# Dummy products in planned idle time, port locks for table steps, and new seeds in an attention and expert-layer kernel

## The chip, the cores and the metric

The kernel runs on one core of a Trainium2 chip. The metric is the device time of one execution in microseconds (us). Three runs of the kernel before took 742.20, 740.81 and 737.13 us: the median is 740.81. The core has TensorE (PE, matrix products into the eight PSUM banks), VectorE (DVE), ScalarE (ACT), GpSimd (POOL) and SyncE (SP, which here issues most DMAs).

## The reference

Four batches of 576 tokens go through windowed attention (8 heads of 64, each token sees itself and the 63 before it), then through a layer of eight experts of which each token takes one, then through a dense layer with a tanh form:

```python
scores = scale * np.matmul(q, k.transpose(0, 1, 3, 2))       # q, k, v: (4, 8, 576, 64)
mask = (rel >= 0) & (rel < 64)
attn = softmax(np.where(mask, scores, -1e9)); x = np.matmul(attn, v)   # -> (2304, 512)
logits = x @ w_gate + modality_bias[modality_id]             # 8 experts
e_idx = np.argmax(logits, axis=1); gate_w = softmax(logits)[e_idx]
for e in range(8):                                           # tokens of expert e
    out[mask] = gate_w[mask, None] * (np.maximum(x[mask] @ w1[e], 0.0) @ w2[e])
h = out @ w_in                                               # (512, 2048)
y = (h - np.tanh(h)) @ w_out
```

## The kernel before

**Attention.** The 32 heads are handled as 16 pairs, four of each batch, and a tail per batch for the last 64 tokens. For each pair PE transposes keys and queries (L618), writes the mask and the scores into two banks (L731, L744), DVE takes row maxima (`nm`, L811), ACT the exponentials (`P`, L818), PE transposes them (L769) and multiplies with the values (L783). ACT or DVE copy each step's result out of PSUM.

**Routing.** After a batch's attention `route` computes the gate logits (L940), their maximum and its index, ranks of the tokens within their expert (L996 to L1000), and scales the token rows (`xr`, L921 and L923), which SP writes to memory (`xs`, L907). One-hot matrices `ob` and `rhs` are multiplied (L1068), and DVE adds the product to the table `T` of token numbers (L1076). `early_table` (after batches 0 and 2) and `unit_table` (after batch 3) turn counts into lists of work units by some dozens of DVE steps on one partition (L1118 to L1252).

**Expert stream.** Five units of up to 504 tokens follow. Units 0 and 1 are two lists of the expert that is the largest in batch 0, and start before attention has ended. For each, POOL gathers the rows (`xg`, L1349), PE transposes them (L618 with `xg`), ACT and DVE split them into two parts `xh` and `xl`; SP loads the weights (`raw`, L1415 and L1421), which are split into `wh` (ACT, POOL or DVE) and `wl` (DVE, at times POOL, L1440). The first products are L1465, the second L1485: 96 of each, all on PE.

**Dense layer.** From 326 us on, PE works at the dense layer (L1872 and L1920); its order is fixed by hand and the change does not touch it.

**What sets the order.** Each engine executes its instructions in one fixed order. Up to the end of the expert stream this order comes from a planner, `Flow`, that runs when the kernel is built: each step is an `Op` with an engine, a duration that the planner assumes, the steps that it waits for, the PSUM banks that it may take and a priority. The planner takes step after step, each at the earliest planned time, and the instructions are written out in this order. Where several steps could go, the lowest priority value goes first, plus a pseudo-random `nudge` whose seed is taken from `SEEDS`: one per batch for the priorities 0 to 20, the last for the rest. The time that the plan holds for a step has no effect on the chip: there only the order on each engine and the waits for data, buffers and banks remain.

`Flow.held` keeps a planned DVE step with `lock=True` from overlapping a planned POOL step, and the other way round. Steps without the lock are planned as if DVE and POOL never met:

```python
o = dict(DVE="POOL", POOL="DVE").get(e)
if o is None or (e == "DVE" and not op.lock):
    return t
a, b = self.hold[o]
return b if a < t + op.eng[e] and t < b else t
```

At the kernel's start `warm` puts nine products of the identity `idB` (128x128 with 128x512, L563) on PE while the first loads are under way.

Of the kernel before, what the change touches and what calls it, by code (L numbers as in the profile page):

```python
# [8 lines left out]
F32 = mybir.dt.float32  # L9
# [9 lines left out]
B, H, S, D = 4, 8, 576, 64  # L19
# [21 lines left out]
EB = (0, 2)  # L41
# [13 lines left out]
PACK = {("k", pi) for pi in range(1, LEND - 1)}  # L55
DQ = 0.62
SPACE = 2.0
NUDGE, SEEDS = 1.0, (17, 17, 88, 60, 17)
TURN, STICK = 0.095, 1.0
CONV0 = 14  # L60
CONVT, CONVP = 122.0, 5.1
SLACK = 8.0
# [94 lines left out]
class Flow:  # L157
# [6 lines left out]
    def __init__(self):  # L164
        self.free = dict(PE=5.8, DVE=5.0, ACT=5.0, POOL=8.0, SP=1.6)
        self.wire, self.th, self.n, self.floor = 0.0, [], 0, 0.0
        self.form = "full"
        self.hold = dict(DVE=(0.0, 0.0), POOL=(0.0, 0.0))
        self.bank = [Tok(0.0) for _ in range(8)]

# [46 lines left out]
    def pick(self):  # L217
# [22 lines left out]
        _, s, th = min((x for x in best[e] if x[0] <= lo), key=lambda x: prio(x[2]))  # L240
        return e, s + self.turn(e, th[3]), th

    def run(self):
        while self.th:
            e, s, th = self.pick()
            op, r = th[3], Done()
            r.e, r.s, r.rel = e, s, [g.take() for g in op.rings]
            r.t = s
            if e:
                end = s + op.eng[e]  # L250
                self.free[e] = end
                if e == "PE":
                    self.form = op.form
                if e == "POOL" or (e == "DVE" and op.lock):
                    self.hold[e] = s, end
                r.t = end + self.LAG[e]
                if op.wire:
                    self.wire = max(self.wire, end) + op.wire
                    r.t = self.wire + op.lag
                elif e == "POOL" and op.lag > 2:  # L260
                    r.t = end + op.lag
            else:
                th[4] = s
            if op.bank is not None:
                free = sorted((b for b in op.bank if self.bank[b].t is not None), key=lambda b: self.bank[b].t)
                r.bs = free[: op.nb]
                r.bts = [Tok() for _ in r.bs]
                r.bt = r.bts[0]
                for b, t in zip(r.bs, r.bts):
                    self.bank[b] = t  # L270
            r.tok = Tok(r.t)
            self.step(th, r)


class Kernel:
# [128 lines left out]
    def front(self):  # L404

        nc, f = self.nc, self.flow
# [52 lines left out]
            f.add(self.t_xsplit(i), -1)  # L459
        for n, t in enumerate(ORDER):  # L460
            f.add(self.t_conv(n, t), 1000 + n)
        f.run()
        self.psP_es.close()

# [92 lines left out]
    def behind(self, r):  # L557
        return r.s < self.gathered + 3.0

    def warm(self):  # L560
        ps = self.psP.tile([128, 512], F32, name="bank5").rearrange("p (a b) -> p a b", b=128)
        for i in range(9):
            self.nc.tensor.matmul(  # L563
                ps, self.idB, self.idB[:, None, :].to_broadcast([128, 4, 128]), start=True, stop=True
            )
# [366 lines left out]
    def route(self, b):  # L932
        nc, rt = self.nc, self.rt
        t0, t1, n = RT * b, RT * b + RT, RT
        o0 = (b % 2) * S
        for hf in range(2):
            r = yield Op(("PE", 0.49), self.tks("O", range(5 * b, 5 * b + 5)), bank=self.bankX, form="heads")
            ps = self.bt(r, 128, 288)
# [14 lines left out]
        r = yield Op(("DVE", 0.4), self.tks("P", [(5 * b + p, h) for p in range(4) for h in range(2)]), lock=True)  # L953
# [3 lines left out]
        r = yield Op(("PE", 0.075 * n), toks + [r.tok], bank=self.bankX, nb=2, form="rows")  # L957
        ps = [self.bt(r, 128, n, 64, i=k) for k in range(2)]
# [3 lines left out]
        r = yield Op(("DVE", 0.7), [r.tok], lock=True)  # L962
# [3 lines left out]
        for k in range(2):  # L966
# [4 lines left out]
                op=ALU.mult,  # L971
# [3 lines left out]
        r = yield Op(("DVE", 1.0), lock=True)  # L975
# [4 lines left out]
        r = yield Op(("ACT", 0.28), [r.tok])  # L980
# [3 lines left out]
        r = yield Op(("DVE", 0.95), lock=True)  # L984
# [9 lines left out]
        r = yield Op(("PE", 0.3), [to], bank=self.bankX)  # L994
# [14 lines left out]
        r = yield Op(("DVE", 0.5), [te], lock=True)  # L1009
# [7 lines left out]
        r = yield Op(("DVE", 0.35), [tp], lock=True)  # L1017
# [7 lines left out]
        r = yield Op(("DVE", 1.2), [tp], lock=True)  # L1025
# [5 lines left out]
        a = rt.tile([128, n], F32, name="ra")  # L1031
# [9 lines left out]
        tb = r.tok  # L1041
        ob = rt.tile([128, n, BR], BF16, name="ob")
        obp = rt.tile([128, n, BR], BF16, name="obp")
        sb = [128, n, BR]
        r = yield Op(("DVE", 0.72), [tb])
        nc.vector.tensor_tensor(
            ob, self.iobr[:, None, :].to_broadcast(sb), bm[:, :, None].to_broadcast(sb), op=ALU.is_equal
        )
        r = yield Op(("ACT", 0.72), [r.tok])
        nc.scalar.activation(obp, ob, AF.Copy, scale=self.pcol)  # L1050
        tobp = r.tok
        rhs = rt.tile([128, n, E, NSLOT], BF16, name="rhs")
        sr = [128, E, NSLOT]
        for i in range(n):
            r = yield Op(dict(DVE=0.3, POOL=0.45), bias=dict(DVE=0.6))
            self.eng(r).tensor_tensor(
                rhs[:, i],
                oh[:, i, :, None].to_broadcast(sr),
                eqa[:, i, None, :].to_broadcast(sr),
                op=ALU.mult,  # L1060
            )
        r = yield Op(dict(DVE=0.75, POOL=1.1), [tobp], bias=dict(DVE=0.8))
        self.eng(r).tensor_tensor(ob, ob, self.tbase[:, t0:t1, None].to_broadcast(sb), op=ALU.mult)
        r = yield Op(("PE", 0.14 * n), [r.tok], bank=self.bankX)
        pT, bk = self.bt(r, BR, E * NSLOT), r.bt
# [9 lines left out]
        r = yield Op(("DVE", 0.25), [r.tok])  # L1075
# [32 lines left out]
    def early_table(self, j, tc):  # L1108
# [2 lines left out]
        v = nc.vector  # L1111
        n = yield from self.counts("nA", tc)
        sh = [1, E]
        r = yield Op(("DVE", 1.6 if j == 0 else 0.6))
        t = rt.tile(sh, F32, name="et")
        mx = rt.tile([1, 1], F32, name="emx")
        if j == 0:
# [24 lines left out]
        if j == 0:  # L1142
# [2 lines left out]
                self.ei[0:1, 0:1], engines=[mybir.EngineType.SP], min_val=0, max_val=E - 1,  # L1145
                skip_runtime_bounds_check_because="an index of the eight experts by its making",
            )
        r = yield Op(("DVE", 0.7), [self.tk("TT", EB[j])])
        k = nc.values_load(
            self.ei[0:1, 1 + j : 2 + j], engines=[mybir.EngineType.DVE], min_val=0, max_val=E * NSLOT - CB,  # L1150
            skip_runtime_bounds_check_because="24 times an expert's index and 4 * j or less",
# [12 lines left out]
    def unit_table(self, tc):  # L1164
# [9 lines left out]
            v.tensor_reduce(c, a, op=ALU.add, axis=AX.X)  # L1174
            return c

        yield Op(("DVE", 1.1), prio=-1)
        s = cum(n, "cs0")
        st = rt.tile(sh, F32, name="st")
        v.tensor_tensor(st, s, n, op=ALU.subtract)  # L1180
# [2 lines left out]
        v.tensor_tensor(  # L1183
            g, n[:, :, None].to_broadcast(s3), self.jC[:, None, :].to_broadcast(s3), op=ALU.is_gt
        )
        yield Op(("DVE", 1.3), prio=-1)
        nu = rt.tile(sh, F32, name="nu")
        v.tensor_reduce(nu, g, op=ALU.add, axis=AX.X)
        j0 = rt.tile(sh, F32, name="j0")
# [2 lines left out]
        cu = cum(nu, "cs1")  # L1192
        cj = rt.tile(sh, F32, name="cj")
        v.tensor_tensor(cj, cu, nu, op=ALU.subtract)
        yield Op(("DVE", 1.0), prio=-1)
        v.tensor_tensor(cj, j0, cj, op=ALU.subtract)
        kb = rt.tile(sh, F32, name="kb")
        v.scalar_tensor_tensor(kb, cj, float(CB), self.e24, op0=ALU.mult, op1=ALU.add)
# [4 lines left out]
        v.tensor_tensor(  # L1203
            le, cu[:, None, :].to_broadcast(su), self.u1[:, :, None].to_broadcast(su), op=ALU.is_le
        )
        yield Op(("DVE", 1.2), prio=-1)
        eu = rt.tile([1, NLIST], F32, name="eu")
        v.tensor_reduce(eu, le, op=ALU.add, axis=AX.X)
        v.tensor_scalar(eu, eu, float(E - 1), None, op0=ALU.min)
# [7 lines left out]
        v.tensor_copy(tab[:, 0, :], eu)  # L1217
        for i, (base, step, cap) in enumerate(((kb, self.uB, E * NSLOT - CB), (cb, self.uC, NT))):
            w = le
            r3 = yield Op(("DVE", 1.3), prio=-1)  # L1220
            v.tensor_tensor(w, ou, base[:, None, :].to_broadcast(su), op=ALU.mult)
            r = rt.tile([1, NLIST], F32, name=f"tr{i}")
            v.tensor_reduce(r, w, op=ALU.add, axis=AX.X)
            v.tensor_tensor(r, r, step, op=ALU.add)
            v.tensor_scalar(tab[:, 1 + i, :], r, float(cap), 0.0, op0=ALU.min, op1=ALU.max)
            rs = r
        self.tab = tab
        for m in range(NSTAT):
            yield Op(("SP", 0.6), [r3.tok])
            u = Unit(None, CL if m == NSTAT - 1 else C)  # L1230
            u.e = self.list_reg(slice(m, m + 1), 0)
            x = yield Op(("DVE", 0.7), [self.tk("TT", B - 1)])
            self.unit(NEARLY + m, u, self.list_reg(slice(m, m + 1), 1), self.T, x.t, NRT)
        yield Op(("DVE", 1.8))
        fin = self.cp.tile([1, 2 + NEARLY], I32, name="fin")
        over = rt.tile([1, 1], F32, name="over")
        v.tensor_scalar(over, rs[:, NSTAT - 1 : NSTAT], float(NT - CL), None, op0=ALU.is_lt)
# [9 lines left out]
            v.tensor_scalar(d, r, float(C * j - NT), None, op0=ALU.add)  # L1247
            v.tensor_scalar(fin[:, 1 + j : 2 + j], d, self.evl[:, j : j + 1], float(NT), op0=ALU.mult, op1=ALU.add)
        self.fin = fin
        r = yield Op(("DVE", 0.2))  # L1250
        okB = self.cp.tile([1, 1], BF16, name="okB")
        v.tensor_scalar(okB, over, float(NSTAT), None, op0=ALU.is_le)  # L1252
        self.tk("table").t = r.t
# [823 lines left out]
```

## Time and profile before

| | |
|---|---|
| median of three runs | 740.81 us (737.13 to 742.20) |
| profiled execution | 739.21 us |
| its span, first to last instruction | 737.4 us |
| PE / DVE / ACT / POOL busy | 97% / 78% / 69% / 42% of the span |
| mean granted TensorE clock | 0.985 |
| expert stream's first product | 103.55 us |
| dense layer | from about 326 us to about 730 us |

A time on an engine's row is measured from the span's start. The granted clock is a share of 2.4 GHz: 1.00 is that level, 0.50 is 1.2 GHz, and a mean between them over a stretch says how much of it was spent at each. "Idle before" is time in which the engine had nothing to execute, with what ended it behind the arrow.

### The profile page before, as it was taken

To read this page: it belongs to the slowest core of one execution; us is meant where nothing else is said; L and a number is where in the kernel's file an instruction comes from. 1 tells how busy PE (TensorE), PEld (TensorE's weight loads), DVE (VectorE), ACT (ScalarE), POOL (GpSimd) and SP (SyncE) were. 2 spreads that over 40 slices of the span, in tenths; PEclk is the share of its full clock that TensorE was granted. 3 is DMA by queue.
4 is the path that set the end of the run, shared out by engine and by line. 5 is a ranking of instruction groups with operands and counts; after the bars stand their busy time and mean duration, and the time that the engine had idled before them with its cause. 6 is when DMAs were issued, how large, how long until landed. Compare 5 with 4: busy or idle time off the path is not lost.

```text
span 737.4 us, 15072 instructions
## 1 busy us (share of the span) xinstructions
PE 712.3 (97%) x5235; PEld 617.1 (84%) x5235; DVE 573.3 (78%) x1084; ACT 508.8 (69%) x1255; POOL 306.3 (42%) x359
## 2 busy tenths in 40 slices
PE   7889989899999999999999999999999999999995
PEld 4778777688888888999988899998989999899994
DVE  5887997979899887749999996767677676757663
ACT  5987884547666665748877776676767766767672
POOL 5455655653424322216774452434234333423222
PEclk9998999999999999999999999999999999999998
DMA  9987947687886966640010110101010000001001
GB/s 191 223 190 175 206 130 204 183 240 225 254 263 211 286 211 231 187 111 2 13 33 0 44 37 8 43 12 33 0 44 22 22 15 29 23 1 44 1 1 47
DMA packets 119251, 77.34 MB, mean 105 GB/s; under 512 B 54968, under 2 KB 112332, under 8 KB 119166
## 3 DMA queue, kind: packets, MB, share of 16 engines
q1 hardware_dynamic: 114822, 66.38, 32.6%
q0 software_dynamic: 3264, 9.63, 4.3%
q8 instruction: 43, 0.70, 0.4%
q10 hardware_dynamic: 1080, 0.28, 0.2%
q14 instruction: 42, 0.34, 0.2%
HBM read 62.10 MB, written 14.16 MB: 103 GB/s over the span
## 4 chain that ended last, share of the span: by engine, by line
PE 74%; DVE 12%; issue 4%; DMA 3%; ACT 2%; POOL 2%; SPq 2%; POOLq 0%; DVEq 0%; ACTq 0%
PE ps_q L1920 21%; PE ps_g L1872 21%; PE bank L1485 14%; PE bank L1465 12%; DVE gv L1893 2%; DVE gv L1892 2%; DMA va<-in_v 2%; PE bank L783 1%; PE bank L618 1%; DMA kr<-in_k 1%; DVE nm L811 1%; SPq L530 1%; PE bank L769 1%; DVE gv L1890 1%; ACT gs L1887 1%
## 5 line engine op out<-in xcount | busy, mean ns | idle before, releaser
L1903 POOL TENSOR_TENSOR gl<-gv,gh 128x384 fp32r<-128x384 f32 x95 | 102.4, 1078 | 167.0 <-ACT gh L1902 165.0
L1920 PE MATMUL ps_q<-H,gl 128*128 128x512 f32 x288 | 113.6, 394 | 0.7 <-POOL gl L1903 0.7
L1920 PE MATMUL ps_q<-H,gh 128*128 128x512 f32 x288 | 113.3, 393 | 0.0
L1890 DVE SCALAR_TENSOR_TENSOR gv<-gu,ps_g 128x384 f32<-128x384 f32 x94 | 51.7, 550 | 79.1 <-ACT gt L1885 78.7
L1902 ACT ACTIVATE gh<-gv 128x384 fp32r<-128x384 f32 x96 | 50.2, 523 | 89.1 <-issue 85.5
L1894 DVE COPY_PREDICATED gv<-gm,gt 128x384 f32<-128x384 int32 x96 | 77.7, 809 | 9.9
L1893 DVE SCALAR_TENSOR_TENSOR gv<-gs,gv 128x384 f32<-128x384 f32 x96 | 68.0, 708 | 10.0
L1440 DVE TENSOR_TENSOR wl<-raw,wh 128x512 fp32r<-128x512 f32 x77 | 59.8, 795 | 9.1 <-ACT wh L397 8.7
L1920 PEld LDWEIGHTS ps_q<-H,gl 128*128 128x128 f32 x288 | 54.0, 188 | 15.1 <-POOL gl L1903 2.6
L1886 ACT ACTIVATE gs<-gu,pa 128x384 f32<-128x384 f32 x96 | 59.2, 616 | 8.7 <-DVE gv L1892 8.7
L1887 ACT ACTIVATE gs<-gu,pa 128x384 f32<-128x384 f32 x96 | 58.9, 613 | 7.8 <-DVE gv L1893 7.7
L1892 DVE SCALAR_TENSOR_TENSOR gv<-gs,gv 128x384 f32<-128x384 f32 x96 | 64.0, 666 | 0.0
L1920 PEld LDWEIGHTS ps_q<-H,gh 128*128 128x128 f32 x288 | 54.0, 188 | 8.6 <-ACT gh L1902 0.3
L1889 ACT ACTIVATE gm<-gu,pth 128x384 f32<-128x384 f32 x96 | 58.4, 609 | 0.0
L1891 DVE TENSOR_TENSOR gt<-ps_g,gt 128x384 f32<-128x384 f32 x94 | 51.7, 550 | 0.0
L1884 ACT ACTIVATE gu<-ps_g 128x384 f32<-128x384 f32 x94 | 44.5, 473 | 1.6 <-PE ps_g L1872 1.6
L1885 ACT ACTIVATE gt<-ps_g 128x384 f32<-128x384 f32 x94 | 45.4, 483 | 0.0
L397 ACT ACTIVATE ys<-bank 128x504 f32<-128x504 f32 (+1 forms) x20 | 11.1, 557 | 46.1 <-PE bank L1485 30.3
L397 ACT ACTIVATE wh<-raw 128x512 fp32r<-128x512 f32 x69 | 41.7, 624 | 0.0
L1465 PE MATMUL bank<-xl,wh 128*128 128x504 f32 (+1 forms) x160 | 41.2, 376 | 0.0
L1465 PE MATMUL bank<-xh,wl 128*128 128x504 f32 (+1 forms) x160 | 40.9, 374 | 0.0
L1465 PE MATMUL bank<-xh,wh 128*128 128x504 f32 (+1 forms) x160 | 40.4, 373 | 0.0
(495 smaller groups left out, 2004.4 us busy)
## 6 DMA issues: line engine op xcount, KB each, us to landing
raw<-in_w SPq DMA_DIRECT2D x80, 256.0 KB, 4.3
craw<-in_win SPq DMA_DIRECT2D x16, 512.0 KB, 4.1
craw<-in_wout SPq DMA_DIRECT2D x16, 512.0 KB, 3.8
va<-in_v SPq DMA_DIRECT2D x32, 128.0 KB, 3.2
yd<-ys SPq DMA_DIRECT2D x16, 252.0 KB, 2.7
yr<-yd SPq DMA_DIRECT2D x20, 192.0 KB, 2.8
kr<-in_k SPq DMA_DIRECT2D x11, 256.0 KB, 5.5
qr<-in_q SPq DMA_DIRECT2D x10, 256.0 KB, 5.2
```

Source lines behind the costliest of these rows:

```text
L1440: self.eng(r).tensor_tensor(lo, w, hi.bitcast(F32), op=ALU.subtract)
L1465: nc.tensor.matmul(ps, wt[:, k, :], xt[:, k, :n], start=(k == 0 and q == 0), stop=(k == 3 and q == 2))
L1485: nc.tensor.matmul(ps, wt[:, k % 4, :], h, start=(q == 0), stop=(q == 3 * NF1 - 1))
L1872: nc.tensor.matmul(ps, w[:, c, :], x[:, c, :], start=(c == 0 and i == 0), stop=(c == 3 and i == 2))
L1886: nc.scalar.activation(s1, u, AF.Square, bias=self.pa1)
L1887: nc.scalar.activation(s2, u, AF.Square, bias=self.pa2)
L1890: nc.vector.scalar_tensor_tensor(v, u, cA, ps, op0=ALU.mult, op1=ALU.mult)
L1892: nc.vector.scalar_tensor_tensor(v, s1, b1, v, op0=ALU.add, op1=ALU.mult)
L1893: nc.vector.scalar_tensor_tensor(v, s2, b2, v, op0=ALU.add, op1=ALU.mult)
L1894: nc.vector.copy_predicated(v, m.bitcast(I32), t)
L1903: (nc.vector if last else nc.gpsimd).tensor_tensor(gl, v, gh.bitcast(F32), op=ALU.subtract)
L1920: self.nc.tensor.matmul(self.po[t], g[:, t * 128 : t * 128 + 128], w, start=(f == 0 and i == 0), stop=(f == NF2 - 1 and i == 2),)
```

## The change

The planner, before it places a PE step that would start well after PE is free, now fills the gap with products of the identity, if it is at least two of them long (0.235 us each, after 0.25 us, and not before 12 us of the plan) and a bank is free. `warm` takes the bank and the number. Thirteen steps of the code of routing and of the tables get `lock=True`. The five seeds are others. In the program that comes out, 17 products of the identity are new: seven ahead of the scores of pair 1, eight ahead of pair 0's products with the values, and two ahead of batch 0's counts (the matmul L1101, L1120 in the change). The line numbers of the change are 17 to 19 higher.

```diff
-NUDGE, SEEDS = 1.0, (17, 17, 88, 60, 17)
+NUDGE, SEEDS = 1.0, (13, 688, 798, 735, 373)
 TURN, STICK = 0.095, 1.0
+WARM = 2
...
+    def warm(self, s, op):
+        n = int((s - self.free["PE"] - 0.25) / 0.235)
+        if n < WARM or s < 12.0:
+            return 0
+        own = op.bank or ()
+        free = [b for b in range(8) if self.bank[b].t is not None and self.bank[b].t <= self.free["PE"]]
+        spare = sorted(free, key=lambda b: (b in own, self.bank[b].t))
+        if spare and not (spare[0] in own and sum(b in own for b in free) <= op.nb):
+            b = spare[0]
+            self.fill(b, n)
+            self.bank[b] = Tok(s)
+            self.form = "full"
+            return n
+        return 0
...
+            if e == "PE":
+                self.warm(s, op)
...
-    def warm(self):
-        ps = self.psP.tile([128, 512], F32, name="bank5").rearrange("p (a b) -> p a b", b=128)
-        for i in range(9):
+    def warm(self, b=5, n=9):
+        ps = self.psP.tile([128, 512], F32, name=f"bank{b}").rearrange("p (a b) -> p a b", b=128)
+        for i in range(n):
...
-        r = yield Op(("DVE", 0.72), [tb])
+        r = yield Op(("DVE", 0.72), [tb], lock=True)
...
-            r = yield Op(dict(DVE=0.3, POOL=0.45), bias=dict(DVE=0.6))
+            r = yield Op(dict(DVE=0.3, POOL=0.45), bias=dict(DVE=0.6), lock=True)
...
-        yield Op(("DVE", 1.2), prio=-1)
+        yield Op(("DVE", 1.2), prio=-1, lock=True)
...
-            r3 = yield Op(("DVE", 1.3), prio=-1)
+            r3 = yield Op(("DVE", 1.3), prio=-1, lock=True)
```

The order of the whole planned part is another. Three places of it follow.

PE, the start of attention: behind the transposes of pair 1's queries (`qr_98`) come its mask and scores. Before:

```order
L618 MATMUL bank_313<-idF,qr_98 128x64
L618 MATMUL bank_314<-idF,qr_98 128x64
L731 LDWEIGHTS idB
L731 MATMUL bank_346<-mF,idB 64x512
L731 LDWEIGHTS idB
L731 MATMUL bank_347<-mF,idB 64x512
```

In the change:

```order
L637 MATMUL bank_313<-idF,qr_98 128x64
L637 MATMUL bank_314<-idF,qr_98 128x64
L582 LDWEIGHTS idB
L582 MATMUL bank_350<-idB 128x512
L750 LDWEIGHTS idB
L750 MATMUL bank_358<-mF,idB 64x512
L750 LDWEIGHTS idB
L750 MATMUL bank_359<-mF,idB 64x512
```

The pair of rows L582 stands there seven times in a row; one of them is shown.

DVE, the last table (`unit_table`, after batch 3), around the addition to `T` (`eu`, `em`, `ou`, `tab`, `tr`: one-partition steps of the table). Before:

```order
L1208 TENSOR_REDUCE eu<-le 1x16
L1209 TENSOR_SCALAR eu<-eu 1x16
L1211 TENSOR_SCALAR em<-eu 1x16
L1213 TENSOR_TENSOR ou<-iom_202,em 1x128
L1217 CAST tab<-eu 1x16
L1076 TENSOR_TENSOR T<-T,bank_3159 126x160
L1221 TENSOR_TENSOR le<-ou,kb 1x128
L1223 TENSOR_REDUCE tr_3197<-le 1x16
```

In the change the table's last steps stand ahead of it (`xl` is a split of unit 1's rows, `cva` a step of the dense weights):

```order
L1243 TENSOR_TENSOR tr_3311<-tr_3311,uC 1x16
L1244 TENSOR_SCALAR tab<-tr_3311 1x16
L1421 TENSOR_TENSOR xl<-bank_3178,xh 128x8x64
L1421 TENSOR_TENSOR xl<-bank_3211,xh 128x8x64
L1421 TENSOR_TENSOR xl<-bank_3179,xh 128x8x62
L1421 TENSOR_TENSOR xl<-bank_3212,xh 128x8x62
L1580 TENSOR_SCALAR cva<-cva 128x512
L1582 TENSOR_SCALAR cva<-cva 128x512
L1095 TENSOR_TENSOR T<-T,bank_3339 126x160
```

The addition has moved behind the whole table and behind the split of unit 1's rows. On PE the products that feed it (L1068, L1087 in the change) stood ahead of the transposes of unit 1's rows, and now stand behind them and behind 46 products of unit 0's second layer (L1485, L1504 in the change).

SP, after batch 1's rows (`xs`): loads of values (`va`, two per pair, 32 in all) and the first weights of the stream (`raw`). Before:

```order
L907 DMA xs<-wout0W 128x512
L907 DMA xs<-wout1W 64x512
L530 DMA va<-in_v 128x4x64 x2
L1415 ISA
L1415 DMA raw<-in_w 128x4x128
```

In the change:

```order
L926 DMA xs<-wout0W 128x512
L926 DMA xs<-wout2W 64x512
L1434 ISA
L1434 DMA raw<-in_w 128x4x128
L1434 ISA
L1434 DMA raw<-in_w 128x4x128
L549 DMA va<-in_v 128x4x64 x2
L1434 ISA
```

Before, the first weight tile stands behind the last pair's values; in the change two tiles stand ahead of the values of the last two pairs. On PE the first eight products of the stream (L1465, L1484 in the change) moved the same way: 48 products with values of three pairs, one group of 16 transposes of `P`, batch 3's tail scores, one rank step and 32 transposes of token rows stood ahead of them and now stand behind.

## Rows read from the trace of the kernel before

**Rows 1.** Windows by stage: length; PE, PEld, DVE, ACT, POOL busy; clock, DMA, GB/s.

```profile
0.00:40.00 40.00, 32.95 (x715) 24.89 (x717) 27.59 (x80) 30.15 (x137) 18.97 (x62) 1.00 0.97 209
40.00:93.00 53.00, 48.48 (x1058) 40.61 (x1054) 45.74 (x134) 45.45 (x199) 30.18 (x52) 0.90 0.85 187
93.00:104.00 11.00, 9.07 (x173) 8.16 (x167) 10.07 (x32) 9.27 (x28) 3.47 (x8) 0.84 0.48 133
104.00:138.00 34.00, 34.00 (x313) 25.26 (x311) 28.61 (x69) 20.86 (x64) 25.04 (x35) 1.00 0.64 184
138.00:146.00 8.00, 5.15 (x43) 4.18 (x43) 7.15 (x25) 3.13 (x6) 2.71 (x3) 0.79 0.61 183
146.00:326.00 180.00, 180.00 (x938) 151.27 (x937) 149.71 (x254) 110.52 (x208) 61.32 (x50) 1.00 0.73 225
326.00:730.00 404.00, 402.60 (x2020) 362.77 (x2018) 304.39 (x494) 289.40 (x618) 163.03 (x148) 1.00 0.07 21
```

**Rows 2.** Windows around the four stretches at the lower clock; the same columns.

```profile
53.00:61.00 8.00, 7.41 (x126) 6.23 (x123) 5.42 (x13) 5.29 (x20) 7.94 (x14) 0.57 0.59 163
77.00:81.00 4.00, 4.00 (x67) 3.47 (x71) 3.73 (x12) 3.23 (x9) 3.97 (x6) 0.57 1.26 185
97.00:102.00 5.00, 4.78 (x95) 4.57 (x95) 4.69 (x17) 3.27 (x8) 0.25 (x1) 0.66 0.32 91
142.00:146.00 4.00, 4.00 (x21) 3.17 (x17) 3.28 (x18) 2.13 (x4) 0.00 (x0) 0.57 0.29 86
```

**Rows 3.** Timeline of all engines, 138 to 142 us: start, length, engine, line, tiles.

```profile
138.04 2.71 DVE L1209 TENSOR_SCALAR eu<-eu 1x16 f32<-1x16 f32 x1
138.24 2.48 POOL L1440 TENSOR_TENSOR wl<-raw,wh 128x512 fp32r<-128x512 f32 x2
...
140.78 0.16 DVE L1211 TENSOR_SCALAR em<-eu 1x16 f32<-1x16 f32 x1
...
141.26 0.30 DVE L1076 TENSOR_TENSOR T<-T,bank 126x160 f32<-126x160 f32 x1
...
141.62 0.81 PE L618 MATMUL bank<-idF,xg 62*128 62x62 f32 x15 [2.85 <-DVE T L1076]
```

**Rows 4.** Waits of PE from 93 to 146 us: line, waited for, total, times, longest.

```profile
PE bank L996 <- DVE xl L1402: 1.2, 1, 1.2
PE bank L769 <- DVE PT L399: 0.6, 1, 0.6
```

**Rows 5.** Timeline of PE around the stream's first product.

```profile
92.60 0.71 PE L769 MATMUL bank<-idF,P 64*128 64x64 f32 x15 [0.83 <-DVE xT L399]
...
103.55 0.73 PE L1465 MATMUL bank<-xh,wh 128*128 128x504 f32 x2
```

**Rows 6.** Timeline of SP's queue, 86 to 101 us.

```profile
86.89 0.65 SPq L907 DMA_DIRECT2D xs<-wout1W  x1
91.19 1.82 SPq L530 DMA_DIRECT2D va<-in_v  x2
93.23 2.09 SPq L1415 DMA_DIRECT2D raw<-in_w  x4
```

**Rows 7.** Timeline of ACT: the first weight tile's split.

```profile
99.77 0.62 ACT L397 ACTIVATE wh<-raw 128x512 fp32r<-128x512 f32 x1
```

**Rows 8.** Timeline of PE: pair 1's scores, and a 512-column product with its follower.

```profile
10.37 1.40 PE L744 MATMUL bank<-kT,qT 64*64 64x128 f32 x32 [0.40 <-ACT kT L397]
...
22.42 0.39 PE L834 MATMUL bank<-mG,idB 128*128 128x512 bf16 x1
22.64 1.05 PE L838 MATMUL bank<-kTt,qbt 128*128 128x128 f32 x8
```

**Rows 9.** A DVE line that is locked already: count, shortest/median/longest ns.

```profile
L1012 DVE TENSOR_SCALAR se<-se x4: 171/296/1037, 49.1 to 125.6; 128x5 f32<-128x5 f32 x4
```

**Rows 10.** Timeline of POOL and PE: unit 2's gather and its transposes.

```profile
148.41 1.03 POOL L1349 DMA_INDIRECT xg<-xs,ids  x1 [0.49 <-issue]
...
188.34 1.21 PE L618 MATMUL bank<-idF,xg 64*128 64x64 f32 x32
```

More of the change, by code (lines that the diff above doesn't have):

```diff
@@ L166, in __init__ @@
         self.wire, self.th, self.n, self.floor = 0.0, [], 0, 0.0
-        self.form = "full"
+        self.form, self.fill = "full", None
         self.hold = dict(DVE=(0.0, 0.0), POOL=(0.0, 0.0))
@@ L461, in front @@
             f.add(self.t_conv(n, t), 1000 + n)
+        f.fill = self.warm
         f.run()
@@ L1061, in route @@
             )
-        r = yield Op(dict(DVE=0.75, POOL=1.1), [tobp], bias=dict(DVE=0.8))
+        r = yield Op(dict(DVE=0.75, POOL=1.1), [tobp], bias=dict(DVE=0.8), lock=True)
         self.eng(r).tensor_tensor(ob, ob, self.tbase[:, t0:t1, None].to_broadcast(sb), op=ALU.mult)
@@ L1113, in early_table @@
         sh = [1, E]
-        r = yield Op(("DVE", 1.6 if j == 0 else 0.6))
+        r = yield Op(("DVE", 1.6 if j == 0 else 0.6), lock=True)
         t = rt.tile(sh, F32, name="et")
@@ L1147, in early_table @@
             )
-        r = yield Op(("DVE", 0.7), [self.tk("TT", EB[j])])
+        r = yield Op(("DVE", 0.7), [self.tk("TT", EB[j])], lock=True)
         k = nc.values_load(
@@ L1175, in cum @@
             return c
-        yield Op(("DVE", 1.1), prio=-1)
+        yield Op(("DVE", 1.1), prio=-1, lock=True)
         s = cum(n, "cs0")
@@ L1185, in unit_table @@
         )
-        yield Op(("DVE", 1.3), prio=-1)
+        yield Op(("DVE", 1.3), prio=-1, lock=True)
         nu = rt.tile(sh, F32, name="nu")
@@ L1194, in unit_table @@
         v.tensor_tensor(cj, cu, nu, op=ALU.subtract)
-        yield Op(("DVE", 1.0), prio=-1)
+        yield Op(("DVE", 1.0), prio=-1, lock=True)
         v.tensor_tensor(cj, j0, cj, op=ALU.subtract)
@@ L1231, in unit_table @@
             u.e = self.list_reg(slice(m, m + 1), 0)
-            x = yield Op(("DVE", 0.7), [self.tk("TT", B - 1)])
+            x = yield Op(("DVE", 0.7), [self.tk("TT", B - 1)], lock=True)
             self.unit(NEARLY + m, u, self.list_reg(slice(m, m + 1), 1), self.T, x.t, NRT)
-        yield Op(("DVE", 1.8))
+        yield Op(("DVE", 1.8), lock=True)
         fin = self.cp.tile([1, 2 + NEARLY], I32, name="fin")
@@ L1249, in unit_table @@
         self.fin = fin
-        r = yield Op(("DVE", 0.2))
+        r = yield Op(("DVE", 0.2), lock=True)
         okB = self.cp.tile([1, 1], BF16, name="okB")
```

## The prediction

> **What bounds the kernel now.** I read the windows by stage first [rows 1]. PE is busy 180.00 of 180 us from 146 to 326 us and 402.60 of 404 us after that. What the change reorders ends with the expert stream, so the time can only move by what PE loses ahead of 146 us: idle time, and time at the lower clock. Idle are 7.05 us up to 40 us, 4.52 us from 40 to 93, 1.93 us from 93 to 104, nothing from 104 to 138 and 2.85 us from 138 to 146 [rows 1] (length less PE busy). The windows around the lower clock come next [rows 2]: a mean of 0.57 over 8 us is 8 x 0.43 x 2 = 6.88 us at half, and half of that, 3.44 us, is what it costs. In the same way the other three cost 1.72, 1.70 and 1.72 us. Together 8.58 us.
>
> The last of these losses has one cause [rows 3]. POOL starts two `wl` steps at 138.24, and the DVE step `eu`, 16 numbers on one partition, takes 2.71 us where its neighbour `em` takes 0.16. Behind it on DVE stands the addition to `T`, which frees the PSUM bank that PE needs for the second half of unit 1's transposes: PE waits 2.85 us and then runs at 1.2 GHz for 3.44 us.
>
> The loss from 93 to 104 us is PE waiting for DVE: for `xT` 0.83 us (it begins ahead of 93) [rows 5], `PT` 0.6, and 1.2 us put down to `xl` [rows 4], with DVE busy 10.07 of 11 us [rows 1]. PE has nothing else in its order there. The stream's products, which could fill it, begin only at 103.55 [rows 5], since the first weight tile is issued at 93.23, behind the last values' load at 91.19, though the row stores ahead of that end at 86.89 + 0.65 = 87.54 [rows 6].
>
> **The change, part by part.** The sum goes against the profiled execution, 739.21 us: a span of 737.4 and 1.8 us around it. It lies 1.6 us under the median of 740.81 and inside the three runs.
>
> *The addition to `T` moves* behind the table and behind 46 products of unit 0's second layer, and its products behind the transposes of unit 1. So the wait of 2.85 us has no cause left, nor the 1.72 us of clock behind it: -4.57 us. The ends are -4.57 and 0 (another wait in the same place). I take the whole, since PE's next 46 products need only hidden tiles and weights. What is late instead: unit 2's gather, which needs `T`. At the stream's mean of 180 us / 938 matmuls = 0.19 us [rows 1], 46 products are 9 us; the gather begins at 148.41 and its rows are transposed at 188.34 [rows 10], so 30 us of slack cover it: 0. Without that cover it would cost up to 9 us.
>
> *The stream's first products move ahead* of three pairs' value products and some routing. With `raw` ahead of the last two values' loads, the first tile can be issued at 87.54. From issue to the end of its split it took 99.77 + 0.62 - 93.23 = 7.16 us [rows 6, 7]: ready at 94.7. PE comes to this place after the transposes of `P`, 92.60 + 0.71 = 93.3 [rows 5], and waits 1.4 us. Behind the eight products the three value groups, which waited, find their inputs ready. Of the 1.93 us idle and 1.70 us of clock I keep 1.4 us as loss: -2.23 us. The ends are -3.63 and, as a gain, 0; past that lies a rival.
>
> *The 17 identity products.* A 512-column product has its follower 0.22 us later (22.42 to 22.64) [rows 8], so they are 17 x 0.22 = 3.74 us of PE. Were all in idle time, they would cost 0; were none, 3.74. The first seven, 1.54 us, stand where pair 1's scores waited 0.40 us [rows 8], so they push them by up to 1.1 us, while ACT has pair 0's exponentials to do; fifteen of 17 stand in the first 40 us, in which PE idles 7.05 us [rows 1]. I take +0.5. They bring no clock there: it is 1.00 over those 40 us.
>
> *The locks* act in the plan alone. L1012 was locked before, and took 171 to 1037 ns [rows 9]: planned apart, it met POOL all the same. I price them at 0 beyond the order they helped to make; the ends are -2.55 us (2.71 - 0.16, which the first term already holds) and +2.55 (the same block elsewhere). The Trainium skill, "SBUF — State Buffer", section "Who interferes with whom", says of the port pair that VectorE and GpSimd share that issue order, not the shape of an operation, decides who blocks. By that rule a lock in a plan is worth nothing once the real starts drift from it; the trace agrees in that row.
>
> *The new seeds* reorder attention up to 93 us. No row prices an order that was not run. The losses from 40 to 93 us are 4.52 idle and 3.44 + 1.72 of clock: a better order can take up to about half, -4.8, a worse one add as much. Taken: 0.
>
> *Less slack on DVE.* From 93 to 146 us DVE is busy 10.07 + 28.61 + 7.15 = 45.83 of 53 us [rows 1]. With 6.8 us less, and 2.55 us less blocked, it is 43.28 of 46.2, 94%. Some of the gain comes back as new short waits. Bounds are 0, as from 104 to 138 us with DVE at 84% and no idle, and 6.8, all of it. I take 1.5, nearer to the first, since PE has stream products to put between.
>
> Sum: 739.21 - 4.57 - 2.23 + 0.5 + 1.5 = 734.41, or **734.4 us**, 0.6% under the profiled execution.
>
> **The rivals.**
>
> *Slower: the stream's first products block attention.* PE executes in order, so if the first weight tile is late, the three pairs' value products behind it wait too. If it is ready no earlier than now, at 100.39, PE waits 100.39 - 93.3 = 7.1 us in place of 1.4, and loses 1.72 us of clock as it did after 141.62: 734.41 + 5.7 + 1.72 = 741.8. With the clock lost, it decides the sign from a wait of 4.5 us on. For it: two tiles only are ahead of the values, whose load waits for a buffer that the blocked products free. Against it: eight products need one tile, and the tile has no such wait. Chance 0.17.
>
> *The locks do not hold and DVE is the bound.* A block of 2.55 us as at 138.04 falls on a step that feeds PE, and the clock falls after it: 734.41 + 2.55 + 1.72 = 738.7, no change. For it: POOL still has scalings and `wl` steps at the table, and the locked row above. Against it: PE has 46 products that wait for none of the table. Chance 0.20.
>
> *More: the lower clock of attention goes too*, by the order or by the identity products: 734.41 - 3.44 - 1.72 = 729.2. Against it: only two of the products stand near either stretch, at the counts of batch 0. The Trainium skill, "TensorE: Matmul & The Clock Gate", Part 1, says that the throttled state is the default and activity releases it. By that rule products without use in the idle time ahead of 53 us would keep the higher level, and the time would be this one's. The trace bears it out so far that each of the four stretches follows idle time, but not that 0.44 us of products is enough. Chance 0.17.
>
> **How the numbers follow.** The forecast itself, 731.5 to 737, has 0.46. The range is 728.5 to 743: it holds the forecast, the second rival, most of the third and the first up to a wait of 8 us, with the seeds' 4.8 us either way in part; 0.2 is left outside. A measurement of this kernel tells about 1% from no change, 7.4 us on 740.81: below 733.4 and above 748.2. Faster: 0.15 of the third rival's 0.17 and 0.18 of the forecast's 0.46, 0.33. Slower: the far end of the first rival with a worse attention, 0.06. Same: 0.61.
>
> **What the profile after would show.** Right: no PE wait above 1 us between 138 and 146 us of before, no clock below 1.00 after the stream's start, its first product near 95 us, the addition to `T` some 10 us later against the second layer's start, and the dense layer starting near 321 us. Wrong, step by step: a PE wait for `wh` or `raw` in front of the stream's first products (first rival); a DVE table step of over 2 us with PE waiting behind it (second); clock at 1.00 from 40 to 93 us (third). The whole is wrong if the stream starts at the same time with the same idle behind it, or if attention's losses up to 93 us differ by more than 5 us from 9.7.

## The result, and the profile after

The changed kernel takes **733.45 us** (median of 6 runs, 732.31 to 734.59); the kernel before, on the same chip, 741.71 us (6 runs, 737.13 to 742.2). The ratio is **0.9899, 95% interval 0.9874 to 0.9925**. The forecast was 734.4 us in a range of 728.5 to 743. The gain of 1.0% lies on the bound between "faster by over 1%" (0.33) and "within 1%" (0.61). The profiled execution took 733.9 us: a span of 732.1 and 1.8 around it, against 737.4 [rows 1].

Windows of the kernel after, with the columns of [rows 1]: length, busy time of PE, PEld, DVE, ACT and POOL, TensorE's granted clock, DMA share, GB/s.

```profile
0.00:40.00 40.00, 33.48 (x680) 24.53 (x682) 26.83 (x80) 28.59 (x127) 18.66 (x62) 1.00 0.98 212
40.00:93.00 53.00, 49.58 (x1114) 40.40 (x1109) 50.52 (x149) 45.00 (x194) 30.81 (x55) 0.97 0.86 202
93.00:104.00 11.00, 11.00 (x143) 8.54 (x142) 9.80 (x32) 10.45 (x39) 4.92 (x9) 1.00 0.54 158
104.00:138.00 34.00, 34.00 (x362) 25.13 (x362) 23.58 (x61) 19.61 (x53) 20.42 (x27) 1.00 0.57 171
138.00:146.00 8.00, 7.39 (x33) 5.86 (x32) 7.59 (x18) 2.70 (x6) 5.97 (x7) 1.00 0.45 149
146.00:320.00 174.00, 172.63 (x897) 144.95 (x897) 155.28 (x265) 108.82 (x204) 61.41 (x48) 0.99 0.77 230
...
45.00:49.00 4.00, 3.12 (x42) 2.10 (x41) 3.76 (x15) 4.00 (x23) 2.46 (x6) 1.00 0.36 80
49.00:53.00 4.00, 4.00 (x79) 3.71 (x75) 4.00 (x11) 3.15 (x13) 4.00 (x8) 0.57 0.59 221
...
148.00:152.00 4.00, 4.00 (x15) 3.27 (x13) 3.36 (x12) 1.11 (x2) 1.06 (x1) 0.57 0.07 19
```

Length less PE busy gives the idle time. From 93 to 104 us it went from 1.93 us to nothing, from 40 to 93 from 4.52 to 3.42, and up to 40 us from 7.05 to 6.52. The wait of 2.85 us on `T`'s addition [rows 3] became one of 1.98 us (0.61 us of it shows in the row of 138 to 146, the rest in the next). Together that is 16.35 us idle in the first 150 us before and 11.92 after. Where [rows 2] has 17.1 us at half clock (1.2 GHz), there are now two stretches of 3.4 us.

PE's timeline around the stream's first product, which was at 103.55 us [rows 5]: start, length, engine, line.

```profile
92.35 0.71 PE L788 MATMUL bank<-idF,P 64*128 64x64 f32 x16
92.99 1.18 PE L1484 MATMUL bank<-xh,wh 128*128 128x504 f32 x4
94.01 1.08 PE L1484 MATMUL bank<-xl,wh 128*128 128x504 f32 x4
95.02 0.45 PE L802 MATMUL bank<-PT,va 128*64 128x64 f32 x8
```

No row has a wait in brackets: the first weight tile was there, and the value products behind the eight stream products lost nothing.

The table's stretch, from the timelines of DVE, POOL and PE of the kernel after. It answers to [rows 3].

```profile
138.33 2.43 DVE L1191 TENSOR_TENSOR le<-upto,nu 1x64 f32<-1x64 f32 x1
...
146.65 2.43 DVE L1421 TENSOR_TENSOR xl<-bank,xh 128x512 fp32r<-128x512 f32 x4
...
149.79 0.31 DVE L1095 TENSOR_TENSOR T<-T,bank 126x160 f32<-126x160 f32 x1
...
138.23 1.19 POOL L940 TENSOR_TENSOR wout2W<-wout2W,heads 64x256 f32<-64x256 f32 x2
139.39 1.29 POOL L1459 TENSOR_TENSOR wl<-raw,wh 128x512 fp32r<-128x512 f32 x1
...
147.37 0.23 PE L1087 MATMUL bank<-rhs,ob 128*126 128x160 bf16 x1 [1.98 <-DVE xl L1421]
```

This is the old stall turned round. A table step of 64 numbers, locked in the plan, still takes 2.43 us while POOL runs a `wout2W` and a `wl` step back to back; the table as a whole ends late; now `xl` stands behind the table, and `T`'s products need the bank that `xl` frees, where before the transposes needed the one that `T`'s addition freed. (Of the 46 second-layer products ahead of `T`'s products, 34 stand behind the transposes of unit 1's rows.)

The dense layer's first product came at 322.9 us instead of 326.3, and from its first to its last product it took 401.0 us instead of 402.5; two waits for `gl`, 0.7 us of the 1.5, were gone. This was in no term, and it is not the change's: each of the fourteen profiles below has one of these two lengths, with either order. The changed kernel's order without its products has 402.5 us again, with two waits for `gl`; the new seeds alone, which gain nothing, have 401.0 without them.

### The profile page after: what moved, and what is told of

Same layout as the page of the kernel before. It is cut to its first block, busy times and chain, and to the rows that moved or that the text cites. A ratio compares the mean times of both kernels' runs of the same rounds, so it can differ in the third digit from the quotient of the medians.

```text
span 732.1 us, 15084 instructions
## 1 busy us (share of the span) xinstructions
PE 712.3 (97%) x5252; PEld 614.9 (84%) x5252; DVE 572.6 (78%) x1095; ACT 504.3 (69%) x1237; POOL 308.8 (42%) x356
## 4 chain that ended last, share of the span: by engine, by line
PE 86%; DVE 5%; DMA 3%; ACT 2%; SPq 1%; issue 1%; POOL 1%; POOLq 0%; DVEq 0%; ACTq 0%
PE ps_g L1891 27%; PE ps_q L1939 26%; PE bank L1484 14%; PE bank L1504 13%; DMA va<-in_v 2%; PE bank L637 2%; ACT P L837 1%; PE bank L802 1%; PE bank L788 1%; DMA kr<-in_k 1%; PE bank L763 1%; SPq L549 1%; PE ps_q L1891 1%; DVE nm L830 1%; ACT PT L415 0%
## 5 line engine op out<-in xcount | busy, mean ns | idle before, releaser
L1912 DVE SCALAR_TENSOR_TENSOR gv<-gs,gv 128x384 f32<-128x384 f32 x96 | 66.3, 691 | 10.7 <-DVE gv L1911 0.9
L1939 PEld LDWEIGHTS ps_q<-H,gl 128*128 128x128 f32 x288 | 54.0, 188 | 13.3 <-POOL gl L1922 0.7
L1911 DVE SCALAR_TENSOR_TENSOR gv<-gs,gv 128x384 f32<-128x384 f32 x96 | 60.8, 633 | 0.0
L1484 PE MATMUL bank<-xl,wh 128*128 128x504 f32 (+1 forms) x160 | 41.0, 375 | 0.0
L1484 PE MATMUL bank<-xh,wh 128*128 128x504 f32 (+1 forms) x160 | 41.0, 375 | 0.0
L1484 PE MATMUL bank<-xh,wl 128*128 128x504 f32 (+1 forms) x160 | 40.8, 374 | 0.0
```

What stands on the lines that cost most here:

```text
L1484: nc.tensor.matmul(ps, wt[:, k, :], xt[:, k, :n], start=(k == 0 and q == 0), stop=(k == 3 and q == 2))
L1911: nc.vector.scalar_tensor_tensor(v, s1, b1, v, op0=ALU.add, op1=ALU.mult)
L1912: nc.vector.scalar_tensor_tensor(v, s2, b2, v, op0=ALU.add, op1=ALU.mult)
L1939: self.nc.tensor.matmul(self.po[t], g[:, t * 128 : t * 128 + 128], w, start=(f == 0 and i == 0), stop=(f == NF2 - 1 and i == 2),)
```

## The experiments

Theory: the gain is the new order of PE's work, which leaves less idle time and so less half clock. Rivals: the identity products hold the clock; the locks remove the blocks; the seeds are all of it. All ratios are to runs of the kernel before on the same chip.

**Without the products** (the plan and every engine's order stay; only the 17 products are missing):

```
-        f.fill = self.warm
+        f.fill = lambda b, n: None
```

> The changed kernel with its plan and its order as they are, without the 17 identity products. Theory 1 (the gain is the new order of TensorE's work; the products only occupy idle time): the time stays at the changed kernel's 733.45 us, between 732 and 735, the first stream product stays within 0.5 us of 93.0 us, and the half-clock stretches are the same two, near 49 and 148 us. Theory 2 (the products hold the clock): TensorE falls to half clock at one or more places near 13 to 22 and 46 us where it did not before, each for about 3.4 us and so worth 1.7 us: 735 to 739 us. Theory 3 (the products cost what they take, 17 x 0.22 = 3.7 us): about 730 us.

733.74 us, ratio 0.9904 (0.9869 to 0.9938): the time of the changed kernel. Yet the clock fell at a place of the products. PE's timeline of this kernel, and its window:

```profile
10.96 1.10 PE L763 MATMUL bank<-kT,qT 64*64 64x128 f32 x32 [1.40 <-DVE kT L417]
...
14.39 0.34 PE L802 MATMUL bank<-PT,va 128*64 128x64 f32 x4 [1.18 <-DVE PT L417]
...
17.00 1.90 PE L763 MATMUL bank<-cvw 64*64 64x128 f32 x32
...
15.00:19.00 4.00, 3.93 (x68) 3.31 (x70) 0.03 (x1) 2.01 (x10) 1.80 (x4) 0.57 0.94 196
```

Where seven and eight products had stood, PE now waits 1.40 and 1.18 us, and the clock falls: 32 scores take 1.90 us, where those at 10.96 us took 1.10. None of the three profiles of this order with products (the changed kernel's two, and that of six for two, below) has a stretch there, so theory 2 was probably right about the place; it was wrong about the price. The first gate logits come at 37.3 us, against 37.5 with the products, which had taken in path time what the clock gave back.

**The new seeds alone** on the kernel before:

```
-NUDGE, SEEDS = 1.0, (17, 17, 88, 60, 17)
+NUDGE, SEEDS = 1.0, (13, 688, 798, 735, 373)
```

> The kernel before with the new seeds and nothing else. Its order puts xg's products ahead of T's. Theory 1 (order): the wait of xg on T's addition (2.85 us) and the half clock behind it (1.7 us) go, and T's own products may wait for the bank that xl frees, 0 to 3.7 us: 737 to 741 us, ratio to before 0.993 to 0.999. Theory 2 (it takes the locks in the plan to remove the wait): 741 us or more. Theory 3 (the seeds alone are the whole change): 733.5 us, ratio 0.989.

741.83 us, ratio 1.0008 (0.9989 to 1.0028). Theory 2's number by another mechanism: `xg` no longer waits for `T`, but `T`'s products wait 5.86 us for `xl`, more than the 3.7 us allowed for.

**The locks alone** (old seeds; only the plan's `lock=True`):

```
-        yield Op(("DVE", 1.1), prio=-1)
+        yield Op(("DVE", 1.1), prio=-1, lock=True)
...
```

> The kernel before with the locks in the plan, the old seeds and no identity products beyond the first nine. Its order has T's products ahead of xg's, but 34 products of the stream stand between them (7.5 us, where before had 10, 2.2 us). Theory 1 (order): T's addition is done by then, so the wait of 2.85 us and its half clock of 1.7 us go: 737 us, ratio 0.994, and in the trace a table step of VectorE still takes over 2 us beside a weight step of GpSimd. Theory 2 (the locks hold on the chip): no step of the table takes over 1 us, and the time is 733 to 736 us. Theory 3 (locks cost VectorE time in the plan): 742 us or more.

743.22 us, ratio 1.0021 (0.9999 to 1.0043): theory 3's number. The trace refutes theory 2. Timelines of DVE, POOL and PE:

```profile
134.81 5.17 DVE L1213 TENSOR_TENSOR cj<-cs,nu 1x8 f32<-1x8 f32 x1
139.91 0.30 DVE L1095 TENSOR_TENSOR T<-T,bank 126x160 f32<-126x160 f32 x1
...
135.00 4.96 POOL L1459 TENSOR_TENSOR wl<-raw,wh 128x512 fp32r<-128x512 f32 x4
...
136.31 2.05 PE L1484 MATMUL bank<-xh,wl 128*128 128x504 f32 x4 [2.55 <-POOL wl L1459]
```

A subtraction of eight numbers, 0.16 us in the kernel after, took 5.17 us beside four `wl` steps in a row. The 34 stream products do cover `T`'s addition; a weight tile and `T`'s own products (2.44 us) are waited for instead.

**Five products alone** (the filling code on the kernel before; PE's order else unchanged):

```
+            if e == "PE":
+                self.warm(s, op)
...
```

> The kernel before with the filling code alone: five identity products, three ahead of a group of scores and two ahead of a transposition near 88 us; order otherwise as before. Theory 1 (order): the time of the kernel before, 741.7 us, within 1.2 us (5 x 0.22 us at most on the path), ratio 0.999 to 1.002. Theory 2 (products hold the clock): one or two of the half-clock stretches near 53 to 61, 77 and 98 us go, 1.7 us each: 738 to 740 us, ratio 0.995 to 0.998.

740.31 us, ratio 0.9992 (0.9974 to 1.001): theory 1, though the interval reaches into theory 2. Its profile has 10.2 us at half clock, before's 17.1; how little one profile says of that, the next run tells.

**The kernel before again.**

> The kernel before, unchanged, as a control. Ratio 1.000, within 0.3%. Its profile tells how far the places of half clock and the waits of one execution repeat: by every theory the four stretches (53 to 61, 77, 98 and 142 us) and the wait of 2.85 us on T's addition stand there again, to 0.3 us.

Ratio 1.0004 (0.9974 to 1.0035). The wait of 2.85 us on `T` came again, the clock's stretches did not. Windows as in [rows 2]:

```profile
53.00:61.00 8.00, 7.81 (x135) 6.59 (x133) 5.66 (x13) 5.37 (x19) 7.94 (x14) 0.60 0.51 144
77.00:81.00 4.00, 3.76 (x79) 2.89 (x82) 3.77 (x15) 3.76 (x11) 3.91 (x6) 1.00 1.30 194
97.00:101.00 4.00, 3.53 (x72) 3.44 (x71) 3.69 (x15) 2.56 (x6) 0.26 (x1) 0.57 0.37 107
```

The one at 77 us is missing. So the four losses of clock that the prediction read off were one draw of an execution, and the runs of this kernel spread from 736 to 747 us.

**The two `wl` steps taken off POOL** in the kernel before, which is the cause that the prediction named for its largest term:

```
-        r = yield Op(by, [r.tok], [R["wl"]], bias=dict(POOL=LATE if i else 0.0), lock=True)
+        r = yield Op(by, [r.tok], [R["wl"]], bias=dict(POOL=LATE if i else 99.0 * (s > 8)), lock=True)
```

> The kernel before, with the last weight tiles' low parts of the first unit kept off GpSimd (the two wl steps at 138.24 us of [rows 3]); the order of VectorE up to T's addition is the same. Theory 1 (the step of 2.71 us is one of 0.15 us that waits for GpSimd's two wl steps, and T's addition stands behind it): that step takes 0.15 to 0.3 us, the wait of 2.85 us is gone or below 0.4 us, no half clock follows near 142 us: 4.6 us less, 737.1 us, ratio 0.994. Theory 2 (xg would wait for something else next, such as xh or a bank): the wait goes but only 0 to 2 us are gained, ratio 0.997 to 1.000.

739.1 us, ratio 0.9973 (0.9951 to 0.9996). Timelines of DVE and PE, and two waits of PE from 125 to 150 us:

```profile
143.95 0.26 DVE L1209 TENSOR_SCALAR eu<-eu 1x16 f32<-1x16 f32 x1
...
PE bank L1485 <- DVE wl L1440: 0.7, 1, 0.7
PE bank L618 <- DVE T L1076: 0.4, 1, 0.4
...
80.17 5.18 DVE L826 TENSOR_TENSOR P<-P,rc 128x512 f32<-128x512 f32 x1
...
85.41 0.69 PE L618 MATMUL bank<-idF,P 64*128 64x64 f32 x8 [5.02 <-DVE P L826]
```

The mechanism is shown: without the `wl` steps the step takes 0.26 us and the wait is 0.4. Its price is not 4.57 us but about 2.0 (0.3 to 3.6), as theory 2 had it, and `wl`, now on DVE, is waited for. The last two rows are chance: the engines' orders at 80 us are those of before, yet in this execution a step of attention met a run of POOL steps and PE lost 5 us.

**`T`'s products placed later** in the changed kernel (table steps at the prices that its trace shows):

```
-        yield Op(("DVE", 1.3), prio=-1, lock=True)
+        yield Op(("DVE", 3.7), prio=-1, lock=True)
...
-        yield Op(("DVE", 1.2), prio=-1, lock=True)
+        yield Op(("DVE", 2.6), prio=-1, lock=True)
```

> The changed kernel, with two table steps priced in the plan at what its trace shows (3.7 us in place of 1.3, 2.6 in place of 1.2), so that T's products stand behind 50 products of the stream in place of 34, 3.5 us later. Theory 1 (the wait of 1.98 us at 147.4 us and the half clock after it are only T's products coming too early): both go, 3.7 us less than the changed kernel: 729.8 us, ratio to before 0.984. Theory 2 (what T frees comes later and the gather is needed): the time does not fall, 733 us or more. Theory 3 (the wait goes, the half clock comes elsewhere): 731.5 us.

734.25 us, ratio 0.9921 (0.989 to 0.9951), no gain over the changed kernel that can be measured, as theory 2 said. Its profile has a span of 730.8 us: the wait of 1.98 us is gone, and PE's waits from 140 to 325 us are these.

```profile
PE bank L1504 <- ACT hh L1515: 1.7, 1, 1.7
PE bank L1504 <- ACT wh L415: 0.3, 1, 0.3
```

The wait came back in another place, at 309.9 us.

**Six products in place of two** at the first batch's count, in the changed kernel:

```
-            self.fill(b, n)
+            self.fill(b, 6 if n == 2 else n)
```

> The changed kernel with six identity products in place of two at its last place, ahead of the first batch's count near 46 us, so that TensorE has no idle time of 0.8 us there; the plan and the order are the same. Theory 1 (idle time is what the clock falls on, and products fill it): the wait of 0.82 us at 48.4 us falls below 0.3 us, the half-clock stretch from 49.3 us goes or moves, and the time falls by 1.7 us to 731.8 us. Theory 2 (the products don't hold the clock): the stretch stays and the time is 733.5 to 734.4 us (4 x 0.22 us at most).

733.4 us, ratio 0.9907 (0.9877 to 0.9937). Windows of this kernel:

```profile
27.00:31.00 4.00, 4.00 (x55) 3.66 (x55) 2.34 (x6) 2.18 (x11) 1.20 (x4) 0.57 0.85 143
45.00:49.00 4.00, 4.00 (x60) 2.67 (x53) 3.69 (x15) 4.00 (x24) 1.16 (x4) 1.00 0.75 149
49.00:53.00 4.00, 3.24 (x81) 2.80 (x79) 3.92 (x11) 3.78 (x17) 3.86 (x7) 1.00 0.13 50
```

The idle time is filled (4.00 of 4 us, 3.12 before the edit) and the clock stays up behind it, as theory 1 said; it fell at 27 us instead, and the time is theory 2's. Nor is the mean clock of its six runs above that of the changed kernel's (0.993 and 0.995).

What is left is which parts the gain needs. Ahead of the stream's first product stand 192 products of P times V (twelve pairs of heads) in the changed kernel and its variants, and 224 or 240 (fourteen or fifteen pairs) in every other order above.

**The changed kernel again.**

> The changed kernel, unchanged, as a control beside the next three, and as a second profile of it. Ratio to before 0.990, within 0.3%. Theory 1 (order): TensorE is idle for about 12 us of the first 150 us again (11.9 in the first profile; 16 to 20 in every order that gave no gain), with 3 to 10 us of half clock whose places differ from the first profile. Theory 2 (each place of half clock belongs to its wait): the same two stretches, near 49 and 148 us.

733.62 us, ratio 0.9906 (0.9882 to 0.9931); idle 11.93 us. Theory 2 falls, and my 3 to 10 us of half clock too: this execution has none in the first 200 us. PE's timeline and a window behind its longest wait:

```profile
146.85 0.23 PE L1087 MATMUL bank<-rhs,ob 128*126 128x160 bf16 x1 [1.98 <-DVE xl L1421]
...
148.00:152.00 4.00, 4.00 (x19) 3.27 (x18) 3.35 (x11) 1.12 (x2) 1.54 (x2) 1.00 0.06 8
```

The same wait of 1.98 us as in the first profile, and the clock at 1.00 behind it, where that had 0.57. The Trainium skill, "TensorE: Matmul & The Clock Gate", Part 1, makes activity release the throttled state; the two executions, with the same instructions and the same wait, show that this alone does not tell whether a given wait is followed by half clock.

**Seeds and locks** (`WARM = 10**6`, so that the plan places no product), **seeds and products** (no locks), **locks and products** (old seeds).

> New seeds and locks, but the plan places no identity product beyond the first nine. In its order only 192 products of P times V stand ahead of the stream's first product, as in the changed kernel (before: 240). Theory 1 (the gain is an order in which the stream begins inside the attention): 732 to 736 us, ratio 0.988 to 0.994, with TensorE idle for 11 to 14 us of the first 150 us. Theory 2 (all three parts are needed): 741 us, ratio 0.998 to 1.002. Theory 3 (any order that the plan draws is as good as another, and the changed kernel's was picked by its time): between the two, 735 to 740 us.

735.23 us, ratio 0.9921 (0.9893 to 0.9948), idle 14.2 us, just past theory 1's bound of 14: theory 1 by the ratio, though the time touches theory 3's 735 to 740 too.

> New seeds and identity products (28 beyond the first nine), without the locks. In its order 240 products of P times V stand ahead of the stream's first product, as before the change. Theory 1 (order): no gain, 739 to 742 us, ratio 0.997 to 1.002, TensorE idle for 15 us or more of the first 150 us. Theory 2 (products hold the clock): at most 7 us of half clock in the profile and 736 to 738 us.

745.49 us, ratio 1.0068 (1.0039 to 1.0097): slower than any theory. It has 30 products (two of them behind the stream's first product), 6.6 us at 0.22, and `xg` waits for `T` as before the change, longer. Its half clock, 13.7 us, is not theory 2's 7 either. PE's waits:

```profile
PE bank L637 <- DVE T L1095: 3.9, 1, 3.9
PE bank L637 <- DVE xl L1421: 1.3, 1, 1.3
```

> The changed kernel with the old seeds: locks and 44 identity products beyond the first nine. In its order 240 products of P times V stand ahead of the stream's first product. Theory 1 (order): no gain, 740 to 744 us, ratio 0.999 to 1.004. Theory 2 (products hold the clock): less than 7 us of half clock in the profile where the locks alone had 17, and 735 to 739 us.

744.29 us, ratio 1.0053 (1.0033 to 1.0073): theory 1, just past its upper end. Every engine has the order of the locks alone but for the products, 33 of which stand behind the stream's first product, so this is a clean pair. The half clock is 10.2 us for 17.1 (one profile each): the locks alone have a stretch of 10.2 us from 131 us, which is not there with the products, 27 of which stand at that place. The mean clock of ten runs each is 0.992 for 0.987. Still the kernel is 0.3% slower (1.0053 against 1.0021), some 2.4 us.

All profiles in one table. Idle is PE's from 0 to 320 us, and "93 to 150" what of it lies there; half is the time at half clock, summed over windows of 1 us up to 200 us; products are 0.22 us each; lost is idle + half / 2 + products. The clock is the mean granted clock over all runs of the kernel, profiled or not (of the kernel before, the 64 runs beside the others).

| kernel | first stream product | idle | 93 to 150 | half | products | lost | span | clock | ratio |
|---|---|---|---|---|---|---|---|---|---|
| after | 93.0 | 11.9 | 2.0 | 6.8 | 3.7 | 19.0 | 732.1 | 0.995 | 0.9899 |
| after, again | 92.5 | 11.9 | 2.0 | 0 | 3.7 | 15.6 | 730.1 | 0.995 | 0.9906 |
| without products | 93.1 | 13.6 | 2.0 | 10.3 | 0 | 18.7 | 732.4 | 0.993 | 0.9904 |
| six for two | 93.6 | 10.8 | 2.0 | 3.4 | 4.6 | 17.1 | 730.3 | 0.993 | 0.9907 |
| `T` later | 92.8 | 10.9 | 0 | 3.4 | 3.7 | 16.3 | 730.8 | 0.994 | 0.9921 |
| seeds, locks | 91.9 | 14.6 | 1.0 | 10.2 | 0 | 19.7 | 734.8 | 0.994 | 0.9921 |
| before | 103.5 | 16.4 | 4.8 | 17.1 | 0 | 24.9 | 737.4 | 0.987 | 1 |
| before, again | 103.5 | 17.5 | 5.5 | 13.7 | 0 | 24.4 | 738.4 | 0.986 | 1.0004 |
| five products | 100.7 | 15.6 | 5.5 | 10.2 | 1.1 | 21.8 | 736.5 | 0.988 | 0.9992 |
| no `wl` on POOL | 108.0 | 19.2 | 4.2 | 13.6 | 0 | 26.0 | 739.3 | 0.989 | 0.9973 |
| seeds | 102.2 | 20.7 | 6.1 | 20.5 | 0 | 30.9 | 740.8 | 0.986 | 1.0008 |
| locks | 102.7 | 20.2 | 7.5 | 17.1 | 0 | 28.7 | 741.4 | 0.987 | 1.0021 |
| locks, products | 104.0 | 14.9 | 1.9 | 10.2 | 9.7 | 29.7 | 743.4 | 0.992 | 1.0053 |
| seeds, products | 107.4 | 16.9 | 7.4 | 13.7 | 6.6 | 30.4 | 742.1 | 0.989 | 1.0068 |

The span less what is lost is 709.9 to 715.1 us in all fourteen, so the sum explains the spans to about 3 us. Every order in which the stream begins near 93 us gains 0.8 to 1.0%; none in which it begins after 100 us gains more than 0.3%. These are three orders (the changed kernel's, `T` later, seeds with locks) against five. What divides them is the idle time from 93 to 150 us: 0 to 2.0 us in the orders that gain, 4.2 to 7.5 in the others, but for locks with products, where 33 products (7.3 us) fill it. Ahead of 93 us they don't differ in this way (8.8 to 13.3 us idle against 9.6 to 14.2). That the early start is the cause is likely, since PE has something to do where attention waits, but no run moved the stream's start alone. Nor did one draw other seeds with the locks, so whether the locks do more than change what the seeds draw is open too.

The clock of the runs says how much of the gain is clock. On the chip of the last four kernels, the changed kernel's four runs have 0.992 to 0.998 and fifteen of the kernel before 0.983 to 0.991. The share below 1.00 times the span is 3.8 us on the mean against 9.3: by this estimate 5.4 us of the 7.4 between the medians are clock, and less idle time, net of the products, is the rest.

## Why the prediction was right, point by point

The time was right, 734.4 against 733.45 us, and so in the main was its idea, that PE's losses ahead of 146 us are what there is to gain: of the 5.3 us between the two profiled spans 3.5 lie ahead of the dense layer, and 1.5 are the dense layer's two lengths. That the number came so close is luck in two ways. Errors in its terms cancelled: in these profiles the term for `T` fell short by 3.7 us, and the one for the seeds, taken at 0, gave 4.5. And the gain is 8.3 us by the medians, where the sum takes 4.8 off a profiled execution that lies 2.5 us under the median of 741.71.

- **The addition to `T`, -4.57: the step failed.** "No cause left" was true of that wait; the end that was named, another wait in the same place, came at 1.98 us: -0.87 us of idle time. And the wait was worth about 2.0 us (0.3 to 3.6) where it was taken away by itself.
- **"Nor the 1.72 us of clock behind it": failed.** A stretch does not belong to its wait, as the second profiles of both kernels show. What held is the sum: three profiles of before's order (before, again, five products) have 17.1, 13.7 and 10.2 us at half clock, four of after's (after, again, without products, six for two) 6.8, 0, 10.3 and 3.4. The means are 13.7 and 5.1, and half the difference is 4.3 us (5.4 by the clock of the runs on one chip), the largest single part of the gain; the sum had 3.4 us of clock in it (1.72 here, 1.70 in the next term).
- **The stream's first products, -2.23: right and too small.** The first came at 93.0 us for a predicted 95, without the 1.4 us of wait that was kept as loss, and all 1.93 us of idle time in that stretch went. It is what all the gaining orders share.
- **The 17 products, +0.5: right within the measurement.** The ratios with them (0.9899, 0.9906) and without (0.9904) are one. The trace adds that they cost path time and give clock back in about equal parts.
- **The locks, 0 beyond the order that they help to make: right on the chip, and that order was worth a great deal.** Steps of the table were blocked for 2.43 us again, and for 5.17 with the locks alone. By the rule of the Trainium skill, "SBUF — State Buffer", section "Who interferes with whom", that issue order decides who blocks, a lock in a plan binds nothing; the trace agrees in those two rows, where a GpSimd step had begun before the VectorE step did. But with the new seeds the locks make the order that gains: 0.9921 with them, 1.0008 without.
- **The seeds up to 93 us, 0 within 4.8: too small, nearly by the whole bound.** From 40 to 93 us 4.5 us of loss went, 1.1 idle and 3.4 of clock: the 9.7 us that the prediction counted there are 5.1 in the first profile after and 4.2 in the second, and the second passes the difference of 5 us that it had set as a sign of being wrong. How much of this is the order can't be told from so few profiles, since the clock is a draw: the kernel before has 8.0 there in its second profile. Nor did it bring the stream's place forward: the transposes of `P` ahead of the stream's start ended at 92.35 + 0.71 = 93.1 us, and at 93.3 before. Idle time from 0 to 93 us fell by 1.6 us, and the products took part of that.
- **Less slack on DVE, +1.5:** the 1.98 us wait is of this kind, behind a DVE that is busy 7.59 of 8 us from 138 to 146. It is also the end that the first term named, so it counts once.

The rivals: the stream's first products did not wait. The locks did not hold, and the block cost a wait behind it, but 738.7 us did not follow, since the stream's start gave more than was counted. The clock of attention went up in part, to 0.97, and in the second profile to 1.00; that execution took 731.8 us, not 729.2. Of the signs of being right two failed: a PE wait of 1.98 us stands at the table, behind a DVE step of 2.43 us as the second rival had it, and in the first profile the clock fell once more after the stream's start, at 148 us.

## What to carry to other kernels

Read the idle time of the engine that bounds the kernel as nearly repeatable (11.9 us in both profiles after, 16.4 and 17.5 before, though a chance block of 5 us occurs) and the clock's fall behind a given wait as a draw: take two profiles before a stretch at half clock is put down to one wait, and compare the mean clock of many runs, which does tell two orders apart. Where a planner sets the order, test the parts of a change together as well as apart: here neither seeds nor locks nor products alone were worth anything that was measured, and two of them together gave nearly all of the gain. Fill idle time with work that is needed, here the next stage's products; products without use kept the clock up at a place and still paid nothing.

## What the runs showed of the hardware that was not expected

- The same instructions with the same wait of 1.98 us were followed by 3.4 us at half clock in one execution and by none in another. The stretches that were seen took 3.4, 6.8 or 10.2 us. The order shows in the mean clock all the same: 0.992 to 0.998 in four runs of the changed kernel against 0.983 to 0.991 in fifteen of the kernel before, on one chip.
- A VectorE step waited for a whole run of GpSimd steps, not for one: 5.17 us beside four `wl` steps of 4.96 us together (it ended at 139.98 us, they at 139.96), and 5.18 us in attention. Whether it is caught varies between executions of one order.
